# One adaLN block on one Trainium2 core: first modulation summed on TensorE, second group's norm and transposes placed among the first heads' maxima, first stores reordered

## The chip, the cores and the metric

The program runs on one core of one Trainium2 chip. The metric is device time in microseconds (us) of one execution; lower is better. Before the change the median of three timed runs is 696.45 us (694.09 to 696.74). The profile shown here is of one further execution.

## The reference

For 2048 tokens of width 448, sixteen heads of 28 and a feed-forward width of 1792, in float32:

```python
mod = (_silu(c) @ w_mod).reshape(c.shape[0], 6, 1, -1)
sa, ca, ga, sb, cb, gb = ...
h = _layernorm(x, axis=-1) * (1 + ca) + sa
x = x + ga * _A_ref(h, A_wqkv, A_wo)      # causal attention, window 256
h = _layernorm(x, axis=-1) * (1 + cb) + sb
x = x + gb * _B_ref(h, B_w1, B_b1, B_w2)  # Dense -> Mish -> Dense
```

## The kernel before, in words

Tokens are worked on in four groups of 512. Every float32 product is made of three fast products: each operand is split into a rounded high part and the remainder (tiles `hh` and `hl` for the normalized tokens, `wq` and `wql` for the weights), and a projection of one tile is eleven matmuls (`passes`, lines 210 to 214).

**The start (lines 400 to 503).** SyncE (SP) issues all loads in one queue: the tokens of group 0, the modulation weights `wm` in two halves (columns 0 to 255 and 256 to 447, four pieces each), and the projection weights in three parts. VectorE (DVE) takes the statistics of the norm. GpSimd (POOL) and DVE then form the first modulation: `sums` (lines 405 to 412) multiplies each piece of `wm` by its column of `sT`, the silu of the condition, and adds it to `acc`; `mods` (lines 414 to 419) turns the sum into columns by four matmuls against ones for each half; `mods_out` copies them to `cols`. Meanwhile TensorE (PE) transposes the normalized tokens (line 441), and `warmup` (line 466) fills gaps with matmuls whose result nobody uses: 8 and 12 of them. ScalarE (ACT) and DVE apply `cols` and split (`hT_hi`, `hT_lo`), and 33 matmuls on line 486 make the first three tiles of q and k, which are stored to DRAM (`scr`). The modulation of the second half is made after the first nine of these.

**The first heads' maxima (lines 993 to 1006).** Heads are loaded back from `scr` as `q` and `k` (`L`). `A` (line 646) makes a head's scores for 128 queries into one of two buffers `sA`, and DVE takes their row maximum into `mx` (line 655). A maximum is needed before a unit `B` (line 679), which makes scores again with the maximum folded in and lets ACT take the exponential into `P` (line 700); `PV` (line 702) multiplies by v. `M2` (line 659) transposes the maxima of two heads (`mt`, line 661), DVE splits them (`mr`), and a small DMA writes them into `q`. In the first stretch `A` runs for heads 0 to 3, four times each, between the matmuls of a generator, `fill_main(0)`: the v tiles first, then the tiles 1, 5, 2 and 6 of q and k. Heads 2 and 3 also step `side`, whose first content is the norm of group 1 (`ln1[1]`). DVE works in order, so statistics and normalization stand between the maxima.

**The units (lines 1008 to 1056).** 192 units follow, 48 for each group of queries. Unit u issues `B(u)`, up to two `A` of the next four heads, loads (`load_slot`), and as many matmuls of the generator as `RATE[g]` us of credit pay for; `FRONT[g]` doubles the credit of the first units. In the order that the program takes, units 0 to 10 of group 0 hold no projection matmul, only the four transposed chunks of group 1 (`gen_hT(1)`, four transposes each). At a group's end what is left of the generator is issued in one piece (line 1014). DMAs that wait in `later` are issued one by one in some units; tiles `st` that carry q and k to the stores come from four buffers (tag `qs`).

Of the kernel before, what the change touches and what calls it, by code (L numbers as in the profile page):

```python
# [8 lines left out]
F32 = mybir.dt.float32  # L9
F32R = mybir.dt.float32r  # L10
# [41 lines left out]
def adaln_block(ctx: ExitStack, tc: tile.TileContext, x, wqkv, wo, w1, b1, w2, c, w_mod, out):  # L52
# [32 lines left out]
    def bank(tag, bufs, name):  # L85
        return PS[0].tile([128, 512], F32, name=name, tag=tag, bufs=bufs)
# [20 lines left out]
    acc01 = st0.tile([112, 2, D], F32, name="acc01")  # L107
# [186 lines left out]
    def gen_hT(g):  # L294
        drain(ln1[g])
        hh, hl = HT[g] = new_T(g, mid)
        for ci in range(4):
            p = bank("mm", 2, f"tr{g}{ci}")
# [32 lines left out]
        return cost(m, p.shape[-1])  # L331


    later = []

    def flush():
        while later:
# [8 lines left out]
    def qk_out(g, m, p, st=None):  # L346
        st = st or qk.tile([128, 2, GT], F32R, name=f"st{g}_{m}", tag="qs", bufs=4)
        r0, gs = m * 128, slice(g * GT, (g + 1) * GT)
        qn = min(max(D - r0, 0), 128)

        def hi():
            ACT.activation(st[:, 0], p, AF.Copy)

        def lo():
            DVE.tensor_tensor(st[:, 1], p, st[:, 0].bitcast(F32), op=ALU.subtract)
# [25 lines left out]
        return passes(*HT[g], wq3[:, :, ms], wql[:, :, ms])  # L381

    def gen_qkv(g, tiles):
        first = {"v2": ("sB", 2), "v3": ("sB", 2), 1: ("pv", 1), 5: ("tr", 1)} if g == 0 else {}
        for m in tiles:
            p = bank(*first.get(m, ("mm", 2)), f"qk{g}_{m}")
            if isinstance(m, str):
                t = int(m[1])
                hh, hl = HT[g]
                ts = slice(t * 128, (t + 1) * 128)  # L390
                ps = passes(hh[:, :, ts], hl[:, :, ts], wq3[:, :, VS], wql[:, :, VS])
                w = yield from tile_mms(p[:, 0:D], [(b, a) for a, b in ps])
# [9 lines left out]
    nm0 = qk.tile([128, 4], F32, name="nma0")  # L402
    XS[0] = [xin0[:, t] for t in range(4)]

    def sums(h, ks):
        cs = HALF[h][0]
        for k in ks:
            w, o = wm01[k][:, :, cs], acc01[:, :, cs]
            if k == 0:
                POOL.tensor_scalar(o, w, sT[:, 0:1], None, op0=ALU.mult)  # L410
            else:
                DVE.scalar_tensor_tensor(o, w, sT[:, k:k + 1], o, op0=ALU.mult, op1=ALU.add)

    def mods(h):
        for ci in HALF[h][1]:
            n = 128 if ci < 3 else 64
            for i in range(2):
                PE.matmul(pm[0:n, 4 * i + ci:4 * i + ci + 1], acc01[:, i, ci * 128:ci * 128 + n], ones[:, 0:1],
                          start=True, stop=True, skip_group_check=True)

    def mods_out(h):
        for i in range(2):
            if h == 0:
                DVE.tensor_scalar(cols[:, i, 0:2], pm[:, 4 * i:4 * i + 2], float(i), None, op0=ALU.add)
            else:
                DVE.tensor_scalar(cols[:, i, 2:3], pm[:, 4 * i + 2:4 * i + 3], float(i), None, op0=ALU.add)
                for r0 in (0, 64):
                    DVE.tensor_scalar(cols[r0:r0 + 64, i, 3:4], pm[0:64, 4 * i + 3:4 * i + 4], float(i), None,
                                      op0=ALU.add)

    def wq_split(part, cis, eng):
        c0, c1 = QCOLS[part]
        for ci in cis:
            split_hi(wqs[ci][:, c0:c1], wq3[:, ci, c0:c1], ACT)
        for ci in cis:
            split_lo(wqs[ci][:, c0:c1], wq3[:, ci, c0:c1], wql[:, min(ci, 2), c0:c1], ci, eng)

    def trs_of(cis):
        for t in (0, 2, 1, 3):
            for ci in cis:  # L440
                PE.transpose(trs[ci][:, t * 128:(t + 1) * 128], XS[0][t][:, ci * 128:(ci + 1) * 128], ident)
# [6 lines left out]
    DVE.scalar_tensor_tensor(nm0, mv0[:, :, 0], -1.0, rs0, op0=ALU.mult, op1=ALU.mult)  # L448
    sums(0, (0,))
    for t in (0, 1):  # L450
        ACT.activation(xin0[:, t, 0:D], xin0[:, t, 0:D], AF.Identity, scale=rs0[:, t:t + 1], bias=nm0[:, t:t + 1])
    for t in (2, 3):
        DVE.tensor_scalar(xin0[:, t, 0:D], xin0[:, t, 0:D], mv0[:, t, 0:1], rs0[:, t:t + 1],
                          op0=ALU.subtract, op1=ALU.mult)
    for t in (0, 2, 1, 3):
        dup(XS[0][t])
    sums(1, (0,))
    sums(0, (1, 2, 3))
    pm = bank("sA", 2, "mc01")
    trs = [bank(("sB", "mm")[ci // 2], 2, f"tr0{ci}") for ci in range(4)]  # L460
    hh, hl = HT[0] = new_T(0, mid)
    warm = bank("pv", 1, "warm")

    def warmup(n):
        for _ in range(n):
            PE.matmul(warm[:, 0:384], identr, mask, start=True, stop=True, skip_group_check=True)

    trs_of((0, 1))
    warmup(8)
    mods(0)  # L470
    trs_of((2, 3))
    warmup(12)
    wq_split(0, (0, 1), POOL)
    sums(1, (1, 2))
    mods_out(0)
    for ci in (0, 1):
        hT_hi(trs[ci], ci, hh, 0)
    hT_lo(trs[0], 0, hh, hl, 0)
    sums(1, (3,))
    hT_lo(trs[1], 1, hh, hl, 0)  # L480
    wq_split(0, (2, 3), POOL)
    first = [(m, bank(tag, b, f"qk0_{m}"), qk_passes(0, m)) for m, tag, b in ((0, "pv", 1), (3, "tr", 1), (4, "sA", 2))]
    for lo_n, hi_n in ((0, 3), (3, 6), (6, 9), (9, 11)):
        for m, p, ps in first:
            for n in range(lo_n, hi_n):
                PE.matmul(p, ps[n][1], ps[n][0], start=(n == 0), stop=(n == 10))
        if lo_n == 0:
            mods(1)
            mods_out(1)
            for ci in (2, 3):  # L490
                hT_hi(trs[ci], ci, hh, 0)
                hT_lo(trs[ci], ci, hh, hl, 0)
            wq_split(1, range(4), DVE)
    x_load(1)
    st01 = {}
    for m, p, ps in first:
# [6 lines left out]
    wq_split(2, range(4), POOL)  # L503
    st0_s.close()
    att, att_s = pool("att")

# [398 lines left out]

    def fill_main(g):
        if g == 0:
            yield from gen_qkv(0, VT + (1, 5, 2, 6))
        if g + 1 < NG:
            yield from gen_hT(g + 1)  # L910
# [78 lines left out]
    def fill0(n):  # L989
        for _ in range(n):  # L990
            pipe.step()
            next(fillers[0])
    need({f"v{t}" for t in range(4)}, 0)
    for i in range(4):
        for t in range(4):
            if t % 2 == 0:
                fill0((4, 1, 1, 0)[i] if t == 0 else 1)
            A(i, t)
            if i >= 2:
                side_step(0, False)  # L1000
        if i % 2:
            fill0(1)
            M2(i // 2)
            if i == 1 and 0:
                rest()
            load_slot(3 + i)
            load_slot(4 + i)
    NU = 3 * NS
    credit = 0.0
    for u in range(NU + 7):  # L1010
# [17 lines left out]
        if r in (7, 11) and 4 * q + 4 < NS:  # L1028
            M2(2 * q + 2 + (r == 11))
        for a in range(4):  # L1030
            if (u - (8, 11, 14, 16)[a]) % 12 == 0 and u >= (8, 11, 14, 16)[a]:
                load_slot(4 * ((u - (8, 11, 14, 16)[a]) // 12) + 8 + a)
        if r - 3 in (0, 1) and 0 <= (u - 12 - 3) // 12 < NS // 4:
            (E, E2)[r - 3](q - 1)
        if g < NG:
# [8 lines left out]
            if v > 1:  # L1044
                side_step(g, len(tiles) > 1)
            if later and r in (1, 4, 5, 6, 8, 9):
                later.pop(0)()
        if u == NU:
            drain(fillers[NG - 1], side[1])
# [105 lines left out]
```

## Time and profile before

| what | value |
|---|---|
| median of three runs | 696.45 us (694.09 to 696.74) |
| the profiled execution's own time | 694.23 us |
| its span, first to last instruction | 692.5 us |
| PE busy | 660.0 us, 95% of the span |
| DVE busy | 349.5 us, 50% |
| ACT busy | 279.3 us, 40% |
| POOL busy | 97.4 us, 14% |
| mean granted TensorE clock | 0.978 |

The busy times are shares of the whole span. The change touches the first 140 us and the order around units 96 to 143, so those stretches are read for themselves. A PE that is busy all the time can still be slow: the granted clock is a column of its own.

### The profile page before, as it was taken

The page shows a single profiled execution, that of the slowest core. Times are in us where ns is not written, and L with a number is a line of the kernel's source. Part 1 is how long each engine was busy: PE and PEld are TensorE (multiplying, and loading weights), DVE is VectorE, ACT ScalarE, POOL GpSimd, SP SyncE. Part 2 cuts the span into 40 slices and gives each one's busy share as a digit, 9 for nine tenths or more (in the row PEclk, how much of TensorE's full clock was granted, in tenths as well). Part 3 has the DMA queues.
Part 4 walks back from the last instruction along what each step waited for, and adds up shares of the span by engine and source line. Part 5 has one row for each costly group of instructions (what it writes and reads, how often), then busy time and mean ns, then how long its engine had stood idle before and what let it go on. Part 6 is the DMA issues. An engine that isn't in the chain of part 4 may idle for free.

```text
span 692.5 us, 10958 instructions
## 1 busy us (share of the span) xinstructions
PE 660.0 (95%) x3925; PEld 521.2 (75%) x3925; DVE 349.5 (50%) x944; ACT 279.3 (40%) x478; POOL 97.4 (14%) x148
## 2 busy tenths in 40 slices
PE   4988999999999999999998999999999999999996
PEld 3765766777777677777665788888888888888885
DVE  6855476565578666577678433335133323241112
ACT  2514444474452644345455752342233223322321
POOL 7413000043000300000001064321000000000002
PEclk9995799999999999999999999999999999999999
DMA  8766465656755566446563564103000200010001
GB/s 222 206 183 228 128 194 191 208 143 213 223 174 153 155 203 214 166 125 199 157 198 109 153 194 121 53 1 107 0 1 1 81 27 1 0 41 13 1 1 53
DMA packets 49586, 83.80 MB, mean 121 GB/s; under 512 B 6254, under 2 KB 28028, under 8 KB 49532
## 3 DMA queue, kind: packets, MB, share of 16 engines
q1 hardware_dynamic: 49532, 83.10, 39.5%
q8 instruction: 31, 0.51, 0.3%
q14 instruction: 23, 0.19, 0.1%
HBM read 53.45 MB, written 29.36 MB: 120 GB/s over the span
## 4 chain that ended last, share of the span: by engine, by line
PE 76%; issue 11%; DVE 5%; DMA 5%; ACT 1%; POOL 1%; SPq 1%; POOLq 0%; DVEq 0%; ACTq 0%
PE z L882 16%; PE qk L326 9%; PE sA L653 6%; PE pv L710 6%; PE sB L697 5%; PE qk_v L326 5%; PE wo L326 5%; PE acc L1075 5%; PE acc L1076 5%; PE acc L1074 5%; PE sB L695 4%; DMA k<-scr 3%; DVE junk L655 2%; PE et L721 1%; PE trf L259 1%
## 5 line engine op out<-in xcount | busy, mean ns | idle before, releaser
L655 DVE CUSTOM_DVE_ANT_0 junk<-sA,mask 128x384 bf16<-128x384 f32 (+2 forms) x256 | 135.4, 529 | 95.3 <-PE sA L653 82.7
L700 ACT ACTIVATE P<-sB 128x512 f32<-128x512 f32 (+2 forms) x192 | 109.1, 572 | 140.4 <-PE sB L697 136.7
L890 DVE TENSOR_TENSOR al<-t,ah 128x512 fp32r<-128x512 f32 x56 | 38.8, 692 | 201.0 <-ACT ah L889 201.0
L888 ACT ACTIVATE t<-z,b1c 128x512 f32<-128x512 f32 x56 | 38.5, 687 | 188.2 <-PE z L882 177.3
L653 PE MATMUL sA<-k,q 84*128 84x384 f32 (+2 forms) x256 | 93.1, 373 | 10.4 <-DVE mx L655 7.1
L697 PE MATMUL sB<-q,k 86*128 86x384 f32 (+1 forms) x352 | 92.8, 338 | 1.1 <-DMA q<-mr 1.0
L882 PE MATMUL z<-hhf,w 128*128 128x512 f32 x224 | 89.8, 401 | 0.0
L882 PE MATMUL z<-hlf,w 128*128 128x512 f32 x224 | 88.8, 396 | 0.0
L1074 PE MATMUL acc<-w2h,ah 128*128 128x448 f32 x224 | 82.1, 367 | 0.0
L1075 PE MATMUL acc<-w2l,ah 128*128 128x448 f32 x224 | 82.1, 367 | 0.0
L1076 PE MATMUL acc<-w2h,al 128*128 128x448 f32 x224 | 82.0, 366 | 0.0
L882 PE MATMUL z<-hhf,w1l 128*128 128x512 f32 x168 | 66.4, 395 | 0.0
L653 PEld LDWEIGHTS sA<-k,q 84*128 84x128 f32 x256 | 50.0, 198 | 20.3 <-DVE mx L655 16.6
L695 PEld LDWEIGHTS <-identr 128*128 128x128 bf16 x320 | 22.2, 101 | 53.0 <-issue 50.2
L695 PE MATMUL sB<-fdmask,identr 128*128 128x128 bf16 (+1 forms) x320 | 61.7, 259 | 0.2 <-ACT P L700 0.2
L697 PEld LDWEIGHTS sB<-q,k 86*128 86x128 f32 x352 | 57.4, 200 | 2.2 <-DMA q<-mr 1.2
L710 PE MATMUL pv<-P,v 128*32 128x256 f32 (+2 forms) x704 | 50.8, 403 | 0.0
L882 PEld LDWEIGHTS z<-hlf,w 128*128 128x128 f32 x224 | 42.3, 189 | 9.8
L882 PEld LDWEIGHTS z<-hhf,w 128*128 128x128 f32 x224 | 42.3, 189 | 8.8 <-issue 0.6
L1074 PEld LDWEIGHTS acc<-w2h,ah 128*128 128x128 f32 x224 | 42.1, 188 | 5.3
L1075 PEld LDWEIGHTS acc<-w2l,ah 128*128 128x128 f32 x224 | 42.1, 188 | 5.2
L1076 PEld LDWEIGHTS acc<-w2h,al 128*128 128x128 f32 x224 | 42.0, 188 | 3.6
(152 smaller groups left out, 988.9 us busy)
## 6 DMA issues: line engine op xcount, KB each, us to landing
k<-scr SPq DMA_DIRECT2D x48, 252.0 KB
scr<-st SPq DMA_DIRECT2D x22, 512.0 KB
q<-scr SPq DMA_DIRECT2D x64, 168.0 KB
scr<-st SPq DMA_DIRECT2D x30, 256.0 KB
x<-x1d SPq DMA_DIRECT2D x10, 448.0 KB
xin<-in_A_x_dram SPq DMA_DIRECT2D x8, 448.0 KB
xr<-in_A_x_dram SPq DMA_DIRECT2D x16, 224.0 KB
x1d<-xr SPq DMA_DIRECT2D x16, 224.0 KB
```

The lines of the kernel that those rows point to most:

```text
L326: PE.matmul(p, b, a, start=(n == 0), stop=(n == 10))
L653: PE.matmul(p[:, c0:384], q[0:84, t * 128:(t + 1) * 128], k[0:84, t * 128 + c0:t * 128 + 384], start=True, stop=True)
L655: DVE.tensor_tensor_reduce(out=junk[:, c0:384], in0=p[:, c0:384], in1=mask[:, c0:384], scale=1.0, scalar=-3.0e38, op0=ALU.add, op1=ALU.max ...
L695: PE.matmul(p[:, c:c + n], identr, fdmask[:, m:m + n], start=(i == 0), stop=False, skip_group_check=True)
L697: PE.matmul(p[:, c:c + 128 * (t1 - t0)], k[:, jj * 128:(jj + 1) * 128], q[:, t0 * 128:t1 * 128], start=False, stop=True, skip_group_check= ...
L700: ACT.activation(P[:, c0:], p[:, c0:], AF.Exp, scale=SCALE)
L710: PE.matmul(pvb[q][32 * a:32 * a + 32, t0 * 128:t1 * 128], V[j % NV][:, h + a, :], Pt[4 * w + a][:, c:c + 128 * (t1 - t0)], start=(b == 0 ...
L882: PE.matmul(zb[n], ps[m][1], ps[m][0], start=(m == 0), stop=(m == 10))
L890: DVE.tensor_tensor(al[n], t, ah[n].bitcast(F32), op=ALU.subtract)
L1074: PE.matmul(p, ah[n][:, ts], w2h[f], start=(f == 0), stop=False)
L1075: PE.matmul(p, ah[n][:, ts], w2l[f], start=False, stop=False)
L1076: PE.matmul(p, al[n][:, ts], w2h[f], start=False, stop=(f == NF - 1))
```

## The change

Five things are done.

1. The first modulation is accumulated in PSUM: `mods(h, ks)` multiplies the pieces of `wm` directly by the columns of `sT`, 16 matmuls of one column for each half in place of 4, and `sums` and the tile `acc01` are gone. The matmuls of the second half stand ahead of the first projection. The 20 warming matmuls become 6.
2. ACT normalizes three of the first group's four tiles (two before); the lower parts of the projection weights' second part are made by POOL (DVE before); the first v tile takes its passes in another order.
3. The norm of group 1 is taken on ACT in place of DVE, its statistics stand ahead of the first maximum, and its four chunks (transposes, from buffers of `sB`) stand among the tiles 1, 5, 2 and 6. Group 0's `hh` and `hl` move to the tag `on`.
4. The stores of tile 5 are cut in two, rows 0 to 31 first; stores are flushed inside the first heads' maxima; loads and stores of the units get other slots.
5. `RATE[2]` goes from 0.93 to 0.83 and `FRONT[2]` from 3 to 2: of group 2's matmuls (units 96 to 143), 40 are left to the drain in unit 143 in place of 14.

```diff
-    def sums(h, ks):
-        cs = HALF[h][0]
+    def mods(h, ks):
         for k in ks:
...
-                PE.matmul(pm[0:n, 4 * i + ci:4 * i + ci + 1], acc01[:, i, ci * 128:ci * 128 + n], ones[:, 0:1],
-                          start=True, stop=True, skip_group_check=True)
+                    PE.matmul(pm[h][0:n, 4 * i + ci:4 * i + ci + 1], wm01[k][:, i, ci * 128:ci * 128 + n], sT[:, k:k + 1],
+                              start=(k == i == 0 and ci == HALF[h][1][0]), stop=(k == 3), skip_group_check=True)
...
-    trs_of((0, 1))
-    warmup(8)
-    mods(0)
-    trs_of((2, 3))
-    warmup(12)
+    mods(0, (0, 1))
+    trs_of(0, (0, 1))
+    trs_of(1, (0, 1))
+    mods(0, (2, 3))
+    for t in (2, 3):
+        trs_of(t, (0, 1))
+    for t in range(4):
+        trs_of(t, (2, 3))
...
+    warmup(6)
...
+            if ci == 0 and x == 0:
+                mods(1, range(4))
+                mods_out(1)
...
         def store():
-            later.append(put)
+            later.append(put_first if (g, m) == (0, 5) else put)
...
-            yield from gen_qkv(0, VT + (1, 5, 2, 6))
+            yield from gen_qkv(0, VT)
+            chunk["v"] = 3
+            tiles, chunks = gen_qkv(0, (1, 5, 2, 6)), gen_hT(1)
+            n = 0
+            for _ in tiles:
+                if n in (6, 8, 9, 15):
+                    next(chunks)
+                n += 1
+                yield
...
-    RATE = (0.68, 1.01, 0.93, 0.45)
-    FRONT = (0, 1, 3, 0)
-    ln1 = {g: gen_ln1(g) for g in range(1, NG)}
+    RATE = (0.68, 1.01, 0.83, 0.45)
+    FRONT = (0, 1, 2, 0)
+    ln1 = {g: gen_ln1(g, g == 1) for g in range(1, NG)}
...
+    for _ in range(8):
+        side_step(0, False)
+    fill0(1)
     for i in range(4):
         for t in range(4):
-            if t % 2 == 0:
-                fill0((4, 1, 1, 0)[i] if t == 0 else 1)
             A(i, t)
+            fill0((1, 1, 0, 1)[i])
+            if i * 4 + t < 6 or i * 4 + t == 11:
+                flush()
```

The rows below are the order in which the built program issues instructions on one engine; rows that repeat are counted (x4). First PE from the program's first matmul, before the change: `tr` are transposes of the normalized tokens `xin`, `mc` the modulation's columns.

```order
L441 MATMUL tr_224<-ident,xin_85 128x128
L441 MATMUL tr_225<-ident,xin_85 128x128
...
L466 LDWEIGHTS identr
L466 MATMUL warm<-mask,identr 128x384
...
L418 MATMUL mc_223<-ones,acc_94 128x1 x4
L441 MATMUL tr_226<-ident,xin_85 128x128
...
L486 MATMUL qk_0_290<-hh_228,wq_88 128x512
```

And the same place after it, up to the first projection:

```order
L416 MATMUL mc_218<-sT,wm_0_90 128x1 x4
L416 MATMUL mc_218<-sT,wm_1_91 128x1 x4
L439 MATMUL tr_220<-ident,xin_85 128x128
...
L416 MATMUL mc_218<-sT,wm_2_92 128x1 x4
L416 MATMUL mc_218<-sT,wm_3_93 128x1 x4
...
L466 MATMUL warm<-mask,identr 128x384
L416 MATMUL mc_219<-sT,wm_0_90 128x1 x2
L416 MATMUL mc_219<-sT,wm_0_90 64x1 x2
...
L504 MATMUL qk_0_281<-hh_224,wq_88 128x512
```

PE now starts with the modulation itself, and all of both halves stands ahead of the first projection (`qk_0`).

Next PE around the maxima of heads 2 and 3, before: `sA` are the scores, `qk_6` a tile of group 0's own projection.

```order
L653 MATMUL sA_2_586<-k_2_382,q_1_397 128x384
L653 MATMUL sA_3_592<-k_2_382,q_1_397 128x384
L653 MATMUL sA_0_601<-k_3_383,q_1_397 128x128
L653 MATMUL sA_1_604<-k_3_383,q_1_397 128x256
L326 MATMUL qk_6_562<-hl_229,wq_88 128x512
L326 MATMUL qk_6_562<-hh_228,wq_88 128x512
L326 MATMUL qk_6_562<-hl_229,wq_88 128x512
L653 MATMUL sA_2_612<-k_3_383,q_1_397 128x384
L653 MATMUL sA_3_617<-k_3_383,q_1_397 128x384
L259 MATMUL tr_629<-ident,xin_350 128x128 x4
```

After, from the transpose `mt` of the maxima of heads 0 and 1 on:

```order
L677 MATMUL mt_597<-ident,mx_513 8x128
L669 MATMUL sA_0_609<-k_2_385,q_1_400 128x128
L669 MATMUL sA_1_612<-k_2_385,q_1_400 128x256
L669 MATMUL sA_2_615<-k_2_385,q_1_400 128x384
L669 MATMUL sA_3_618<-k_2_385,q_1_400 128x384
L669 MATMUL sA_0_621<-k_3_386,q_1_400 128x128
L325 MATMUL qk_2_572<-hh_224,wq_88 128x512
L325 MATMUL qk_2_572<-hh_224,wql 128x512
L325 MATMUL qk_2_572<-hl_225,wq_88 128x512
L669 MATMUL sA_1_630<-k_3_386,q_1_400 128x256
L325 MATMUL qk_2_572<-hh_224,wq_88 128x512
```

The transposes of group 1 have left this place; three of its four chunks stand ahead of it. Five scores of heads 2 and 3 follow each other, and projection matmuls stand between the later ones.

Last DVE at the same place, before: `sta` and `mva` are the statistics of group 1, `xin` its normalization, and the row that only reads the accumulated maximum is the one without a source.

```order
L655 ISA junk,mx_567<-sA_2_586,mask 128x384
L655 ISA mx_567 128x1
L219 BN_STATS sta_589<-xin_350 128x6
L220 BN_AGGR mva_571<-sta_589 128x2
L655 ISA junk,mx_567<-sA_3_592,mask 128x384
...
L249 TENSOR_SCALAR xin_350<-xin_350,mva_571,rsa_598 128x448
L655 ISA junk,mx_567<-sA_2_612,mask 128x384
```

After:

```order
L354 TENSOR_TENSOR st_5_566<-qk_5_530,st_5_566 128x512
L679 CAST mr_599<-mt_597 8x128
L680 TENSOR_TENSOR mr_599<-mt_597,mr_599 8x128
L671 ISA junk,mx_608<-sA_0_609,mask 128x128
L671 ISA mx_608 128x1
L671 ISA junk,mx_608<-sA_1_612,mask 128x256
L671 ISA mx_608 128x1
L671 ISA junk,mx_608<-sA_2_615,mask 128x384
```

Statistics and normalization no longer stand between the maxima.

More of the change, by code (lines that the diff above doesn't have):

```diff
@@ L331, in tile_mms @@
         return cost(m, p.shape[-1])
-    later = []
+    later, late = [], []
     def flush():
@@ L357, in store, with put_first @@
         def store():
-            later.append(put)
+            later.append(put_first if (g, m) == (0, 5) else put)
+        def put_first():
+            put_rows(0, 5, st, ((0, 32, 1, 0),))
+            late.append(lambda: put_rows(0, 5, st, ((32, 128, 1, 0),)))
+            done.add((g, m))
         def put():
@@ L383, in gen_qkv @@
     def gen_qkv(g, tiles):
[L384 removed]
+        first = {"v2": ("sB", 2), "v3": ("sB", 2), 1: ("pv", 1), 6: ("pv", 1)} if g == 0 else {}
         for m in tiles:
@@ L403, in adaln_block @@
     XS[0] = [xin0[:, t] for t in range(4)]
-    def sums(h, ks):
-        cs = HALF[h][0]
+    def mods(h, ks):
         for k in ks:
[L408 to L418, printed above, removed]
-                          start=True, stop=True, skip_group_check=True)
+            for ci in HALF[h][1]:
+                n = 128 if ci < 3 else 64
+                for i in range(2):
+                    PE.matmul(pm[h][0:n, 4 * i + ci:4 * i + ci + 1], wm01[k][:, i, ci * 128:ci * 128 + n], sT[:, k:k + 1],
+                              start=(k == i == 0 and ci == HALF[h][1][0]), stop=(k == 3), skip_group_check=True)
     def mods_out(h):
@@ L447, in adaln_block @@
         POOL.tensor_tensor(rs0[:, h], rs0[:, h], mhalf[:, h], op=ALU.pow)
[L448 to L455, printed above, removed]
+    for h in (slice(0, 2), slice(2, 4)):
+        DVE.scalar_tensor_tensor(nm0[:, h], mv0[:, h, 0], -1.0, rs0[:, h], op0=ALU.mult, op1=ALU.mult)
+        for t in range(4)[h]:
+            xn0(t)
+    for t in range(4):
         dup(XS[0][t])
-    sums(1, (0,))
-    sums(0, (1, 2, 3))
-    pm = bank("sA", 2, "mc01")
+    pm = [bank("sA", 2, f"mc{h}") for h in range(2)]
     trs = [bank(("sB", "mm")[ci // 2], 2, f"tr0{ci}") for ci in range(4)]
-    hh, hl = HT[0] = new_T(0, mid)
+    hh, hl = HT[0] = [mid.tile([128, 4, GT], F32R, name=f"h{n}0", tag="on", bufs=2) for n in "hl"]
     warm = bank("pv", 1, "warm")
@@ L502, in adaln_block @@
     put_rows(0, 4, st01[4], ((0, 48, 1, 0),))
-    wq_split(2, range(4), POOL)
+    for c in range(4):
+        if c not in (0, 1, 2, 3):
+            wq_lo(1, c, DVE)
+    for c in range(4):
+        wq_hi(2, c)
+        wq_lo(2, c, POOL)
     st0_s.close()
@@ L1001, in adaln_block @@
         if i % 2:
-            fill0(1)
             M2(i // 2)
-            if i == 1 and 0:
-                rest()
             load_slot(3 + i)
             load_slot(4 + i)
+    later[:0] = late
     NU = 3 * NS
@@ L1043, in adaln_block @@
                 credit -= step(g)
-            if v > 1:
+            if v > 1 and u > 8:
                 side_step(g, len(tiles) > 1)
-            if later and r in (1, 4, 5, 6, 8, 9):
+            if later and r in (1, 3, 4, 5, 6, 9):
                 later.pop(0)()
```

77 lines of the change are left out of this document (45 added, 32 removed).

## The prediction

> **What bounds the kernel now.** I read the page's busy times and slices first, then a table of busy time by stage, then the waits of PE in the weak stage, the chain of waits, and the order of time at the start. The page's first section and its row of granted clock:
>
> ```profile
> PE 660.0 (95%) x3925; PEld 521.2 (75%) x3925; DVE 349.5 (50%) x944; ACT 279.3 (40%) x478; POOL 97.4 (14%) x148
> PEclk9995799999999999999999999999999999999999
> ```
>
> PE bounds the kernel, and the granted clock is low in two of the 40 slices, near the span's tenth. So time is to be won where PE idles or runs slowly, not by taking work from others. Busy time by stage; the columns are the stretch in us, its length, then busy time and instructions of PE, of weight loads (PEld), DVE, ACT and POOL, then PE's granted clock and the DMA:
>
> ```profile
> 10.30:19.40 9.10, 8.55 (x47) 5.83 (x47) 7.56 (x11) 3.80 (x7) 6.51 (x9) 1.00 0.84 220
> 37.20:46.00 8.80, 8.79 (x40) 6.95 (x40) 4.02 (x15) 1.74 (x3) 0.32 (x1) 1.00 0.81 248
> 46.00:50.90 4.90, 3.64 (x16) 2.23 (x14) 3.87 (x15) 0.60 (x1) 0.00 (x0) 1.00 0.13 46
> 50.90:54.30 3.40, 1.60 (x6) 0.98 (x6) 3.19 (x12) 0.15 (x1) 0.32 (x2) 1.00 1.04 375
> 54.30:58.40 4.10, 2.48 (x7) 1.07 (x7) 3.30 (x11) 0.44 (x1) 2.09 (x5) 0.50 0.63 189
> 58.40:78.40 20.00, 19.81 (x88) 14.35 (x86) 9.27 (x39) 11.12 (x20) 5.07 (x4) 0.50 0.38 132
> ```
>
> At 50.9 to 54.3 PE issues 6 matmuls and DVE is busy nearly throughout; then the clock falls to half and stays there to 78.4, although PE shows as busy. The waits of PE from 40 to 62 us (us in total, times, longest):
>
> ```profile
> PE sA L653 <- DVE mx L655: 2.6, 3, 1.5
> PE tr L259 <- DVE xin L249: 1.5, 3, 0.6
> ```
>
> PE waits for the maxima, and these stand behind the statistics and the normalization in DVE's queue. How much the half clock costs is seen in the exponentials of the units, one row of ACT's line 700 for each unit (stretch, length, busy time and count, clock, DMA):
>
> ```profile
> 58.40:78.40 20.00, 5.88 (x12) 0.50 0.38 132
> 78.40:97.00 18.60, 5.89 (x12) 1.00 0.66 200
> 97.00:129.40 32.40, 9.38 (x20) 1.00 0.71 233
> 129.40:136.80 7.40, 2.39 (x4) 1.00 0.27 88
> 136.80:148.30 11.50, 4.59 (x8) 1.00 0.60 155
> ```
>
> Twelve units almost without projection matmuls (four, at the end) take 20.0 us at half clock; the next twelve take 18.6 us with some 35 of them. So that work is nearly free there at full clock.
>
> **The change part by part. The start.** The chain of waits gives the unit prices (start, us, what, count); the projections of tiles 0, 3, 4 (line 486) end and the v tiles begin at 28.32, and v ends at 37.4:
>
> ```profile
> 21.26 0.68 PE mc L418 x8
> 25.02 3.30 PE qk L486 x13
> 28.32 9.08 PE qk_v L326 x44
> 37.40 4.42 PE qk L326 x19
> 45.83 0.56 DVE junk L655
> 46.54 0.56 DVE junk L655
> 53.39 3.16 DMA k<-scr
> 63.82 0.87 PE tr L259 x4
> 136.77 0.44 PE tr L259 x4
> ```
>
> A projection matmul costs 4.42/19 = 0.233 us, a v matmul 9.08/44 = 0.206, a transpose 0.11 at full clock and 0.22 at half. PE's first work in order of time (start, us, what, count):
>
> ```profile
> 12.05 2.11 PE L466 MATMUL warm<-mask,identr 128*128 128x384 bf16 x8
> 14.23 1.05 PE L418 MATMUL mc<-ones,acc 112*128 112x1 f32 x8
> 16.05 2.11 PE L466 MATMUL warm<-mask,identr 128*128 128x384 bf16 x12
> 18.31 0.48 PE L486 MATMUL qk<-hh,wq 128*128 128x512 f32 x1
> ```
>
> The first 8 warming matmuls take as long as the next 12: 0.26 against 0.18 us. PE starts slow here, whatever the clock column shows before the first recorded change. Four modulation matmuls leave 8 records of 0.12 us. They stream one column, so the weight load must set that time, and I let it double with the clock as a transpose does: 0.22. SP issues the second half's pieces of `wm` as the first half's land:
>
> ```profile
> 7.40 0.33 SPq L59 DMA_DIRECT2D wm<-in_w_mod_dram  x1
> 10.16 0.31 SPq L59 DMA_DIRECT2D wm<-in_w_mod_dram  x1
> ```
>
> So after the change PE can begin at 7.4 and no longer waits for sums. But its queue ahead of the first projection is long: 32 records (7.0 us at 0.22), 16 transposes (3.4 at half clock), 6 warming matmuls (2.1 at 0.35, twice the later ones' time) and 32 records of the second half, half of them 64 wide (0.68/8 = 0.085 each at full clock, 0.17 at half: 2.7 to 5.4). That ends at 22.6 to 25.3. The 33 projections take 7.7 us, and some 8 of them run at half clock first (+1.6). The v tiles then begin at 31.9 to 34.6, against 28.3. If the clock is full from the start, the same list gives 3.9 + 1.8 + 1.1 + 2.7 + 7.7 = 17.2 us from 7.4, so 24.6. I take **+5 us (−3.7 to +7)**, nearer the slow end because nothing in that list but six matmuls resembles the work after which the clock rose.
>
> [...]
>
> POOL's four lower parts (about 1.2 us each in place of DVE's) end before the third group of v passes, which the new order of passes puts last; DVE's gain lets the first stores start earlier, but their loads are not waited for. Both are nought; without this cover each is worth under 1 us.
>
> **The heads' maxima, to unit 12.** From the end of v at 37.4 to unit 12 at 78.4 is 41.0 us now. After: 28 projection matmuls (6.5), 8 scores (0.6 a head, 1.2), 12 transposes (1.3) make 9.0 us. Heads 2 and 3 are then bound by DVE. By form, at full clock:
>
> ```profile
> L655 DVE CUSTOM_DVE_ANT_0 junk<-sA,mask 128x384 bf16<-128x384 f32 x32 | 17.7, 554 | 10.3 <-PE sA L653 8.6
> L655 DVE CUSTOM_DVE_ANT_0 junk<-sA,mask 128x256 bf16<-128x256 f32 x8 | 3.4, 420 | 3.3 <-PE sA L653 3.3
> L655 DVE CUSTOM_DVE_ANT_0 junk<-sA,mask 128x128 bf16<-128x128 f32 x8 | 2.3, 288 | 5.0 <-PE sA L653 4.7
> L355 DVE TENSOR_TENSOR st<-qk,st 128x512 fp32r<-128x512 f32 x7 | 4.8, 687 | 0.0
> ```
>
> Two wide maxima start 46.54 − 45.83 = 0.71 apart, 0.16 above the row's 0.55; so a head takes 0.71 × 2 + 0.58 + 0.45 = 2.45, two heads 4.9, and one lower part of a store 0.7 stands ahead: 5.7 us with the turn-round. Twelve units follow; they hold 33 projection matmuls and fewer PV than the twelve at 78.4, so 18.6 − 1.5, and 0.7 for the late maxima of heads 2 and 3: 17.8. Sum 32.5, so **−8.5 us at full clock**.
>
> But five scores follow each other there, and PE does about 0.6 us of work in 2.8. Six matmuls in 3.4 us brought the fall at 54.3; 16 in 4.9 us did not at 50.9. I expect the clock to fall in most executions, and to return soon, since eleven dense projections follow: one stretch like 3.4 us at half clock, worth 1.7, taken as **+1.5 (0 to +11)**. Loads of heads 4 to 7 now stand behind fewer stores; the stores of tile 5 stand behind the maxima of heads 2 and 3, and a load lands 3.2 us after its issue (the DMA row above), about when head 6 is due: 0 (to +2).
>
> **Units 12 to 48.** Now 136.8 − 78.4 = 58.4 us. Group 1's projections end in unit 42 instead of 47, so 31 units at 32.4/20 = 1.6 us and 5 without filler at 11.5/8 = 1.4, less a little since group 0's are narrower: 49.6 + 6.5 = 56. **−2.5 (−4 to 0).**
>
> **Group 2.** 26 more matmuls of 0.206 fall into the drain: +5.3 us there. If the units they leave are bound by PE, these give it back; three more units near 98 to 105 are left without filler. **+0.5 (−1 to +5.3).** Groups 1 and 3 keep their order on PE: 0.
>
> Sum: 5 − 8.5 + 1.5 − 2.5 + 0.5 = −4 us. The profiled execution took 694.23, so **690 us**. That execution is 2.2 us below the median of 696.45. The sum is made against it and not scaled; half a per cent of the median, 3.5 us, is about what a measurement of this kernel can tell from no change.
>
> **The rivals.** (1) PE's clock rises during the new early work. For it: the matmuls begin 3 us sooner. Against: one-column matmuls hardly stream. The start is then −3.7 instead of +5: 690 − 8.7 = 681.
>
> (2) The gain is eaten: the start costs 7, and group 2's drain its 5.3 because the units before it are bound by DVE and ACT. For it: eight units without filler take 11.5 us, hardly less than units with. 690 + 2 + 4.8 = 697. Against: both must be at their ends.
>
> (3) Slower: the clock falls at heads 2 and 3 and stays half through the first twelve units, as it did from 54.3 to 78.4 though PE was busy. Half of a like stretch of 24 us, less the 1 or so already in the sum, is 11 more: 701. It decides by whether units with about 3 projection matmuls each are dense enough; before, units without any were not, and the clock came back 1.6 us after the first such matmuls at 76.7:
>
> ```profile
> 77.09 1.50 PE qk L326 x4
> 78.72 0.23 PE sB L697
> ```
>
> That these matmuls now stand in every unit from the first speaks against it.
>
> [...]
>
> **How the numbers follow.** Forecast 0.57, rival 1 0.14, rival 2 0.20, rival 3 0.09. The forecast's own band is 686 to 694, of which about four fifths lie below 693.0 (faster by over 0.5%): faster 0.61, with rival 1. Same (693.0 to 699.9) is rival 2 and the rest of the forecast: 0.30. Slower is rival 3: 0.09. The range takes in rivals 1 and 2, 681 to 697; rival 3 and tails are left out.
>
> **What would show it.** The exponentials of units 0 and 12 start now, in ACT's order of time, at:
>
> ```profile
> 59.94 0.48 ACT L700 ACTIVATE P<-sB 128x384 f32<-128x384 f32 x1
> 79.04 0.49 ACT L700 ACTIVATE P<-sB 128x384 f32<-128x384 f32 x1 [1.52 <-PE sB L697]
> ```
>
> Right: v begins later than 28.3, the warming rows and the projections show half pace near 20 to 26; those two rows stand near 58 and 77, by the same sum; the clock column holds no 20 us of 0.50. Wrong: v begins before 28 (the start's price), the clock column at half for more than two stretches of 3.4 us between 45 and 75 (the gap), or the stretch of units 96 to 144 longer than now by over 2 us (the drain).

## The result, and the profile after

In 20 executions of each kernel the changed one takes 698.24 us in the median and the kernel before 694.03: ratio 1.0059, 95% interval 1.0035 to 1.0083. It is slower by 0.6%, about 4 us. The forecast was 690 with a range of 681 to 697. The profiled execution of the changed kernel took 697.66 us (span 695.9, against 692.5), so it stands for the median; its difference of 3.4 us is what has to be explained.

The page of the changed kernel, its row of busy times and its row of granted clock:

```profile
PE 664.5 (95%) x3959; PEld 529.4 (76%) x3959; DVE 339.2 (49%) x930; ACT 283.0 (41%) x483; POOL 97.8 (14%) x152
PEclk9899999999999999999998999999999999999999
```

The long stretch of half clock near the span's tenth is gone (5 and 7 before; now 8 or more everywhere), and DVE has 10 us less to do. The first is as forecast; the time still went up. So the next view is one that tells where in the program the distance between the two kernels changes. The exponential of each unit is one row of ACT (line 700 before, 716 after); the table subtracts their start times in the profiled executions.

| unit | before, us | after, us | after minus before |
|---|---|---|---|
| 0 | 59.94 | 59.66 | -0.27 |
| 12 | 79.04 | 77.05 | -1.99 |
| 42 | 126.44 | 124.10 | -2.34 |
| 48 | 136.87 | 130.99 | -5.88 |
| 54 | 145.91 | 143.66 | -2.25 |
| 96 | 226.72 | 224.39 | -2.32 |
| 132 | 294.86 | 289.14 | -5.72 |
| 150 | 326.35 | 328.46 | +2.11 |
| 168 | 354.78 | 356.98 | +2.20 |
| 191 | 387.16 | 391.02 | +3.86 |

Up to unit 48 the change wins nearly 6 us. It loses 3.6 in the next six units, 4.4 between units 96 and 150, and 1.7 behind unit 168. Two rows of ACT's order of time, units 0 and 12 after the change:

```profile
59.66 0.49 ACT L716 ACTIVATE P<-sB 128x384 f32<-128x384 f32 x1 [2.95 <-PE sB L713]
77.05 0.49 ACT L716 ACTIVATE P<-sB 128x384 f32<-128x384 f32 x1 [0.81 <-PE sB L713]
```

**The start.** The chain of waits of the changed kernel (start, us, what, count):

```profile
7.61 3.55 PE mc L416 x16
11.16 0.96 PE tr L439 x4
12.12 3.20 PE mc L416 x16
15.32 2.66 PE tr L439 x12
17.98 1.03 PE warm L466 x6
19.01 3.82 PE mc L416 x32
22.83 9.37 PE qk L504 x29
```

The early modulation matmuls take 0.22 us each and the transposes 0.22, against 0.12 and 0.11 at full clock before: half pace. The warming matmuls take 1.03/6 = 0.17 each, so in this execution they run at full pace from the first, behind 12 transposes (0.18 for the later ones before). The second half's 32 records take 0.12, and then this order of time of PE shows half pace again (0.43 from one projection to the next; the granted clock is 0.50 from 21.4 to 28.2), then full (0.23):

```profile
26.33 0.63 PE L504 MATMUL qk<-hl,wq 128*128 128x512 f32 x1
26.76 0.63 PE L504 MATMUL qk<-hh,wq 128*128 128x512 f32 x1
...
30.66 0.39 PE L504 MATMUL qk<-hl,wq 128*128 128x512 f32 x1
30.89 0.39 PE L504 MATMUL qk<-hh,wq 128*128 128x512 f32 x1
...
32.93 0.36 PE L325 MATMUL qk_v<-wq,hh 128*128 128x448 f32 x1
```

The v tiles begin at 32.93 instead of 28.3.

**The end of group 1's projections.** In the order of time of PE and of the DMA queue (SP) near unit 50:

```profile
134.72 0.34 PE L711 MATMUL sB<-fdmask,identr 128*128 128x128 bf16 x2
134.82 0.48 PE L713 MATMUL sB<-q,k 86*128 86x384 f32 x2
137.25 0.51 PE L669 MATMUL sA<-k,q 84*128 84x384 f32 x1 [1.96 <-DMA k<-scr]
```

```profile
130.97 1.36 SPq L59 DMA_DIRECT2D q<-mr  x2
132.43 0.41 SPq L59 DMA_DIRECT2D q<-scr  x1
132.89 0.38 SPq L59 DMA_DIRECT2D k<-scr  x1
```

The first score of head 21 waits for its load, which is issued at unit 47 behind the rows of the maxima. Units 42 to 48 have no filler left and take 6.89 us instead of 10.43, so the load, unmoved in units, comes too late in time. The clock falls behind the wait, to 0.50 from 137.4 to 140.8; busy time in the stretch (length, PE, weight loads, DVE, ACT, POOL, clock, DMA):

```profile
131.00:137.40 6.40, 4.37 (x41) 2.94 (x39) 3.12 (x10) 5.32 (x9) 2.54 (x2) 1.00 0.48 128
137.40:143.70 6.30, 6.30 (x42) 4.63 (x43) 3.56 (x11) 3.01 (x6) 1.63 (x2) 0.73 0.60 154
```

This is one of several; the waits of PE over the whole span, first before, then after (us in total, times, longest):

```profile
PE sA L653 <- DVE mx L655: 7.1, 13, 1.5
PE sA L653 <- DMA k<-scr: 2.5, 4, 1.1
```

```profile
PE sA L669 <- DMA k<-scr: 8.0, 8, 2.0
PE sA L669 <- DVE mx L671: 5.2, 13, 1.1
```

The maxima are waited for less, the loads more.

**The end of group 2's projections.** The stretches between the exponentials of units 96, 132, 144 and 150, first before, then after:

```profile
226.72:294.86 68.14, 67.03 (x498) 49.94 (x496) 42.25 (x138) 34.05 (x58) 5.52 (x5) 1.00 0.58 185
294.86:318.00 23.14, 22.77 (x182) 17.84 (x183) 17.40 (x52) 9.89 (x19) 0.00 (x0) 1.00 0.51 137
318.00:326.35 8.35, 8.01 (x76) 5.70 (x69) 6.69 (x22) 5.13 (x10) 1.58 (x3) 1.00 0.90 250
```

```profile
224.39:289.14 64.75, 62.48 (x472) 45.41 (x470) 42.67 (x138) 32.70 (x55) 5.49 (x5) 1.00 0.63 195
289.14:317.58 28.44, 28.20 (x207) 22.45 (x209) 16.65 (x50) 11.48 (x20) 0.00 (x0) 1.00 0.41 112
317.58:328.46 10.88, 9.55 (x76) 7.03 (x69) 7.61 (x24) 5.18 (x10) 1.63 (x3) 0.84 0.75 220
```

In the first stretch PE has 26 matmuls fewer and is 3.4 us shorter. The second has 25 more and is 5.3 longer. The third has the same 76 instructions, and is 2.5 longer at a clock of 0.84. What stands at its begin, in PE's order of time after the change:

```profile
316.70 0.37 PE L325 MATMUL wo<-wo,hlo 128*128 128x448 f32 x1
316.91 0.34 PE L711 MATMUL sB<-fdmask,identr 128*128 128x128 bf16 x2
...
320.88 0.44 PE L669 MATMUL sA<-k,q 84*128 84x384 f32 x1 [1.06 <-DVE mx L671]
```

A score waits 1.1 us for a maximum, and the clock drops behind that (0.51 from 321.7 to 325.1). Why DVE is late is seen in its own order of time: it adds each finished tile of the output to rows of `x` (the tile `xr`, line 622), and the maxima stand behind these sums in its queue.

```profile
316.67 0.62 DVE L622 TENSOR_TENSOR xr<-xr,wo 128x448 f32<-128x448 f32 x1 [2.61 <-DMA xr<-in_A_x_dram]
318.88 0.62 DVE L622 TENSOR_TENSOR xr<-xr,wo 128x448 f32<-128x448 f32 x1 [0.71 <-DMA xr<-in_A_x_dram]
320.29 0.53 DVE L671 CUSTOM_DVE_ANT_0 junk<-sA,mask 128x384 bf16<-128x384 f32 x1
```

The 40 projections of unit 143 are most of four output tiles, made in 8.3 us. SP loads the rows of `x` for the last two of them at 311.95 and 316.12, while the row of projections is already running, and DVE waits 3.3 us for them. Before the change no such sum waits for its rows. So this too is a load that has become late.

### The profile page after: what moved, and what is told of

The parts are those of the page before. It is cut to its first block, busy times and chain, and to the rows that moved or that the text cites. A ratio compares the mean times of both kernels' runs of the same rounds, so it can differ in the third digit from the quotient of the medians.

```text
span 695.9 us, 11033 instructions
## 1 busy us (share of the span) xinstructions
PE 664.5 (95%) x3959; PEld 529.4 (76%) x3959; DVE 339.2 (49%) x930; ACT 283.0 (41%) x483; POOL 97.8 (14%) x152
## 4 chain that ended last, share of the span: by engine, by line
PE 74%; issue 11%; DMA 8%; DVE 5%; SPq 1%; ACT 1%; POOL 0%; POOLq 0%; DVEq 0%; ACTq 0%
PE z L898 15%; PE qk L325 9%; PE sA L669 6%; PE pv L726 5%; PE sB L713 5%; PE acc L1102 5%; PE acc L1103 5%; PE acc L1104 5%; DMA k<-scr 4%; PE sB L711 4%; PE qk_v L325 4%; PE wo L325 4%; DVE junk L671 2%; PE mc L416 2%; PE qk L504 1%
## 5 line engine op out<-in xcount | busy, mean ns | idle before, releaser
L713 PE MATMUL sB<-q,k 86*128 86x384 f32 (+1 forms) x352 | 91.1, 334 | 1.6 <-DMA q<-mr 1.6
```

The costliest lines, as they stand in the source:

```text
L713: PE.matmul(p[:, c:c + 128 * (t1 - t0)], k[:, jj * 128:(jj + 1) * 128], q[:, t0 * 128:t1 * 128], start=False, stop=True, skip_group_check= ...
```

## The experiments

Each time is a median, each ratio one to the kernel before on the same chip; that kernel's own median was 693.6 to 694.5 each time. The ratios are not quotients of these medians and can differ from them by up to 0.4%. The changed kernel's 698.24 is from the first occasion, so differences to it carry the spread between occasions too.

**Group 2's two numbers undone.**

```diff
-    RATE = (0.68, 1.01, 0.83, 0.45)
-    FRONT = (0, 1, 2, 0)
+    RATE = (0.68, 1.01, 0.93, 0.45)
+    FRONT = (0, 1, 3, 0)
```

> The changed kernel with group 2's two numbers as they were (RATE 0.93, FRONT 3). Theory A, the drain: the 26 matmuls that the new numbers leave for the end of group 2 cost PE time that the units before them don't give back; by the two profiles units 96 to 150 are 4.4 us longer after the change, so this kernel takes 698.2 - 4.4 = 693.8 us, a ratio of about 1.000 to the kernel before, and the distance to before at unit 150 is -2.3 as at unit 96. Theory B, interaction: the loss belongs to what else has moved (the earlier units, clock windows), and the numbers alone do little: 697 us or more, ratio 1.004 or more.

Measured: 691.25 us, ratio 0.9969 (0.9942 to 0.9996), so 7.0 under the changed kernel. In the profile the distance to before is -1.98 at unit 96 and -2.48 at unit 150, as theory A had it. The two profiled executions are 7.8 us apart: 4.9 of it lies between units 96 and 150, and 3.3 behind unit 168, where this execution shows no half clock. The latter can be chance. The start was 1.7 us earlier at unit 0 (v tiles at 31.45), but nothing of that is left at unit 96.

**The same two numbers alone, in the kernel before.** The edit is the reverse, on the kernel before.

> The kernel before with only group 2's two numbers changed (RATE 0.83, FRONT 2). Theory A: 4.4 us slower, about 698.4 us, ratio 1.006, all of it between the exponentials of units 96 and 150, and some 40 projection matmuls of wo in a row near unit 143. Theory B: under 1.5 us, ratio under 1.002.

Measured: 698.98 us, ratio 1.0072 (1.0037 to 1.0108). Between units 96 and 150 the profile loses 4.3 us (+0.11 to +4.42), in the same pieces as above:

```profile
226.82:291.50 64.68, 62.44 (x472) 45.42 (x470) 42.78 (x138) 32.66 (x55) 5.50 (x5) 1.00 0.61 195
291.50:319.67 28.17, 28.04 (x207) 22.45 (x209) 17.12 (x51) 11.57 (x21) 0.00 (x0) 1.00 0.44 121
319.67:330.76 11.09, 9.58 (x76) 6.42 (x69) 7.15 (x22) 5.16 (x9) 1.63 (x3) 0.85 0.68 198
```

So this part alone costs 4.7 us, with none of the rest of the change present. Theory B falls. Here too DVE stands idle for 2.7 us ahead of the fourth output tile's sum, which starts at 321.14 after a load of `x` issued at 318.42; that it waits for this load is read from the times, since the profile names another releaser.

**The old start in the changed kernel.** Sums on DVE and POOL and 20 warming matmuls, as before, and with them the old norm of group 0 and the lower parts of the weights' second part on DVE; all else as changed.

```diff
-    mods(0, (0, 1))
-    trs_of(0, (0, 1))
...
+    trs_of((0, 1))
+    warmup(8)
+    mods(0)
+    trs_of((2, 3))
+    warmup(12)
```

> The changed kernel with the start of the kernel before (sums on DVE and POOL, 20 warming matmuls), everything else as after the change. Theory A, the price of the start stays where it falls: v tiles begin at 28.3 instead of 32.9, and the 4.6 us reach the end: 693.6 us, ratio 1.000. Rival, given back: the heads' maxima then wait for DVE or for the first loads, so that unit 0 is earlier by less than 2 us and the end by less still: 696.5 us or more, ratio 1.004 or more.

Measured: 694.36 us, ratio 1.0001 (0.9968 to 1.0034), 3.9 under the changed kernel. In its profile unit 0 is 4.5 us earlier than after the change, and 3.4 of them are left at the last unit. The rival falls. Both starts vary with the execution: with the old one the v tiles begin at 27.8 to 30.9 us in the nine profiles of this study that have it, with the new one at 31.5 to 36.1 in four. The 36.1 is an execution (that with the old load units, below) whose clock did not come up behind the transposes: its six warming matmuls take 2.13 us.

**One load a unit earlier.** The second head of each four is loaded at unit 10 of the pattern instead of 11, ahead of the rows of the maxima.

```diff
-            if (u - (8, 11, 15, 15)[a]) % 12 == 0 and u >= (8, 11, 15, 15)[a]:
-                load_slot(4 * ((u - (8, 11, 15, 15)[a]) // 12) + 8 + a)
+            if (u - (8, 10, 15, 15)[a]) % 12 == 0 and u >= (8, 10, 15, 15)[a]:
+                load_slot(4 * ((u - (8, 10, 15, 15)[a]) // 12) + 8 + a)
```

> The changed kernel with every fourth head's second load (heads 9, 13, 17, 21 and so on) one unit earlier. Theory C, the load: units 42 to 48 got shorter by 3.5 us with the change, units 48 to 54 longer by 3.6, since a score waits 2.0 us for k and the clock falls for one 3.4 us stretch behind that wait; with the load a unit (about 1.1 us) earlier the wait falls to about 1 us and the clock may stay full: 1 to 3 us less, 695 to 697 us. Rival: the transfer ends when it did, since its queue or its buffer is not free before, or the time comes back in the next unit: 698 us, no change.

Measured: 690.24 us, ratio 0.9956 (0.9923 to 0.9990): 8 us under the changed kernel (7 by the two ratios), more than any theory had. The waits of PE in this kernel:

```profile
PE sB L713 <- DMA q<-mr: 5.9, 6, 2.0
PE sA L669 <- DVE mx L671: 4.2, 12, 0.7
PE sA L669 <- DMA k<-scr: 0.3, 1, 0.3
```

The waits on k are gone (8.0 to 0.3), those on the maxima's rows, which now stand behind the load, grew (1.6 to 5.9), DVE is waited for 1.0 less: 4.4 in all. One half-clock stretch of 3.4 us fewer (six for seven) is 1.7 more. That makes 6.1 of the 6.3 us between the two profiled executions (697.66 and 691.38); the rest between the medians isn't explained.

By units, the gain does not lie where theory C looked for it. The missing half-clock stretch is one at the start, and 0.8 us are won before unit 0. Units 48 to 54 still take 12.16 us: in place of the wait on k a unit waits 1.5 us for the maxima's rows, and the clock falls behind that as it does after the change, where it is 0.73 in the 6.3 us behind the wait. The largest piece, 2.5 us, comes in units 144 to 150: they take 8.35 us, as in the kernel before, although the row of 40 projections is still there. The second head's load no longer stands in the queue between the maxima's rows and the first output tile's store; the last two loads of `x` are issued 2.8 and 4.5 us behind the first projection of the row (3.4 and 7.6 after the change), and DVE's sums there wait for PE alone:

```profile
DVE xr L622 <- PE wo L325: 3.0, 4, 0.8
```

**Is it the other two loads?** The change also moved the third and fourth heads' loads from units 14 and 16 to 15 and 15; here that alone is undone.

> The changed kernel with the loads of the third and fourth head of each four back at units 14 and 16 (the change has 15 and 15). Theory D: the third head's load, issued a unit later, is what scores wait for (waits of scores on k are 7.3 us in the profile after, 2.5 us before): they fall by 2 us or more and the time to 696 us or less. Rival: the second head's load at unit 11 is the late one, as its move by one unit took all those waits away; the old numbers change nothing: 697 to 699 us.

Measured: 698.78 us, ratio 1.0060 (1.0034 to 1.0086), k still waited for 7.9 us. Theory D falls. After the change the five longest waits on k are all for second heads (21, 33, 37, 57 and 61); with the old units the longest are for heads 21 (2.7 us), 59, 37 and 61. The profiled execution took 702.94 us, the longest of its twelve; against the profile after the change it loses 3.2 us before the v tiles.

**The same earlier load in the kernel before** (10 for 11 in its own list).

> The kernel before with only the second head's load one unit earlier (10 for 11). Theory C2: the late loads came with the change, as units 43 to 50 got free of filler; before, scores waited 2.5 us for k in all, so 1 to 2.5 us less here, 692 to 693.5 us, ratio 0.996 to 0.998, against 0.9897 between the changed kernel and its version with the earlier load (690.24 over the median of 698.24 on another occasion). Rival: the earlier load helps either kernel alike, by other means than those waits: 6 us or more, 688 us or less.

Measured: 693.80 us, ratio 1.0004 (0.9970 to 1.0039). No gain can be told. The load became worth moving only with the change.

**The middle part alone.** The kernel before with the second group's norm and chunks among the maxima, the outputs' buffers for the first chunks, the new order of v's first passes and the order of the first stores; its own start, group 2 numbers and load units.

> The kernel before with only the middle part of the change (second group's norm and chunks among the first heads' maxima, first chunks in the outputs' buffers, order of the first stores); the start, group 2's numbers and the load units are those of before. By the prediction's terms for this part (-8.5, +1.5, -2.5): 694.2 - 9.5 = 684.7 us. Theory A, additive: the changed kernel with the old start took 694.4, less 4.4 for group 2's numbers: 690.0 us, ratio 0.994. Rival: what is won to unit 48 is lost at the next heads' loads, whatever the start: 693 us or more, ratio 0.998 or more.

Measured: 690.83 us, ratio 0.9941 (0.9914 to 0.9968). Additive, to a microsecond. It is 3.7 us faster than before, and not the 9.5 of the prediction's terms: by its profile unit 48 is 9.7 us earlier than before, unit 54 only 6.1, with head 21 waiting 1.9 us for k again. So the rival's mechanism is there too, but it takes back only a part.

**The second half's modulation mixed among the projections** (the changed kernel). What stood behind the 32 records, the copy of their columns and the splits of the last two chunks and of the weights' second part, now stands behind the last of the mixed ones.

```diff
+    mixed = [mods_of(1, range(4))]
...
             for n in range(lo_n, hi_n):
                 PE.matmul(p, ps[n][1], ps[n][0], start=(n == 0), stop=(n == 10))
+                if mixed and next(mixed[0], 0) == 0:
```

> The changed kernel with the second half's 32 one-column records one instruction after each of the first 16 projections of the first tiles, not all ahead of them. Theory E, the clock: the records stream nothing, so with all in a row the clock falls for two stretches (21.4 to 28.2 us) and the projections after them run at half pace; mixed, PE streams about half of the time and the clock stays full: v tiles begin at about 31.6 instead of 32.9 us, since the third chunk then waits some 1.5 us, and the time falls by 1.3 us to about 697. Rival: the clock falls just the same, since half is not enough: v begins at 33 to 35 us, 698 to 700 us.

Measured: 703.42 us, ratio 1.0131 (1.0093 to 1.0169). The v tiles begin at 38.2. Worse than either theory; PE's order of time:

```profile
25.40 0.48 PE L499 MATMUL qk<-hh,wql 128*128 128x512 f32 x1
25.81 0.28 PE L420 MATMUL mc<-sT,wm 112*64 112x1 f32 x2
26.02 0.49 PE L499 MATMUL qk<-hl,wq 128*128 128x512 f32 x1
...
28.10 0.77 PE L499 MATMUL qk<-hl,wq 128*128 128x512 f32 x1
28.81 0.37 PE L420 MATMUL mc<-sT,wm 112*64 112x1 f32 x2
29.11 0.79 PE L499 MATMUL qk<-hh,wq 128*128 128x512 f32 x1
```

and its clock by stretch:

```profile
17.80:27.00 9.20, 9.05 (x45) 5.85 (x44) 2.08 (x3) 0.99 (x3) 2.56 (x3) 1.00 0.87 251
27.00:37.20 10.20, 9.47 (x25) 6.27 (x24) 3.66 (x10) 3.30 (x6) 4.24 (x4) 0.50 0.00 1
```

At full clock a projection and its two records took 0.46 us with records 128 wide, but 0.62 with those 64 wide. Then the clock fell at 27, with PE busy for all but 0.15 of the 9.2 us ahead, and stayed down for 10 us, though from 30.7 on only projections ran, with two waits of 0.4 us for the late splits. Of the delay of v, 0.9 us come from the warming matmuls, which ran at half pace in this execution (2.13 us in place of 1.23). Theory E's remedy falls: the clock fell with the records mixed in as well.

**The combination**: middle part, old start, group 2's old numbers, the earlier load.

> Middle part of the change with the start and group 2's numbers of before, and the second head's load one unit earlier (units 8, 10, 15, 15). Additive: 694.4 - 4.4 - 8.0 = 682.0 us, ratio 0.982. With overlap (part of what the earlier load saved was in group 2's end, which is undone here): 684 to 687. Rival: the waits only change their name, since PE has the same matmuls to do and the maxima's rows then stand behind the load in the queue: 689 us or more.

Measured: 684.78 us, ratio 0.9863 (0.9829 to 0.9897); the case with overlap. It differs from the middle part alone in the loads' units only (8, 10, 15, 15 for 8, 11, 14, 16) and is 6.0 us faster.

**Two small edits on it**, one by one and together: RATE 0.97 for group 2, and the old order of v's first passes.

> The combination (middle part of the change, old start, group 2's numbers of before, second head's load one unit earlier) with RATE 0.97 for group 2: no projection matmul is left for unit 143, against 14 at 0.93 and 40 at 0.83. Theory A, the drain has a price per matmul: 26 more cost 4.4 to 4.7 us, 0.17 us each, so 14 fewer give 2.4 us: 682.4 us, ratio 0.983. Rival, a threshold: the first 14 are hidden beside the exponentials as the scores go on, only a long row stops DVE and ACT: 684 to 685.5, no change.

> The combination with the passes of v's first tile in their old order: with the old start, the new order asks first for the lower part that DVE splits last, and PE waited 0.5 us for it. Theory: 0.5 us less at the v tiles and at the end, 684.3 us, not told from no change in the time, but the wait of qk_v on wq is gone from the profile. Rival: the wait moves to the first stores.

> The combination with both small edits: the passes of v's first tile in their old order and RATE 0.97 for group 2 (no projection matmul left for unit 143). Theory A, a price per drained matmul: 0.5 us of wait and 14 x 0.17 = 2.4 us less than the combination's 684.8: 681.9 us, and units 96 to 150 shorter than the combination's by about 2 us. Threshold rival: units 96 to 150 as in the combination with the old order, about 684 us or as that one measured.

Measured: 682.61 (0.9859, 0.9804 to 0.9913), 682.17 (0.9861, 0.9802 to 0.9920) and 681.88 us (0.9817, 0.9782 to 0.9851); by the medians all three are at 0.983. None of the three can be told from the combination by its interval. The wait of qk_v on wq is gone with the old order. Whether the last 14 drained matmuls have a price stays open: units 96 to 150 take 103.86 us in the combination, 100.70 with RATE 0.97, but 100.02 with the old order of passes alone, which doesn't touch them, and 99.85 with both. The combination's longer time lies in units 96 to 132, where its clock fell for one stretch (at 230.7; projections 0.43 us apart from 231.1 on), not at the drain. The last kernel has the lowest median here, 1.5 to 2.2% under the kernel before by its interval.

## Why the prediction was wrong, point by point

Three steps of the sum failed. Group 2 was put at +0.5 and measured 4.4. Units 48 to 54 had no term and cost 3.6, because loads issued a fixed number of units ahead came late. What lies behind unit 168 had none either and cost 1.7. The terms up to unit 48 came out.

**The start (+5, from -3.7 to +7): right.** 4.6 us in the profile, 3.9 in the experiment, v inside the 31.9 to 34.6. The record prices were right too (0.22 at half pace). Rival 1's time is out. One step inside was off: in the profiled execution the clock was up behind the transposes, since the warming matmuls run at 0.17 at once and not at the 0.35 of the list. But behind the 32 records it was down again, and 13 projections ran at half pace (0.43), not the 8 that the author had estimated. In two other executions the six warming matmuls take 1.7 us in place of 1.2, so the clock came up among them; in the one with the old load units projections run at half pace until 31 us, though the same twelve transposes ran; so the agreement of the start's time is in part luck.

**The maxima, to unit 12 (-8.5 and +1.5): right.** From the v tiles to unit 12 it takes 77.05 - 32.93 = 44.1 us instead of 79.04 - 28.32 = 50.7: -6.6 against -7. Inside, two errors cancel: unit 0 came at 59.66 and not near 58, and the twelve units took 17.4 us and not 19. The clock fell, and for one stretch of 3.4 us (0.50 from 55.5 to 58.9; the profile before has one of that length too, 0.50 from 368.3 to 371.7):

```profile
56.20 0.63 PE L325 MATMUL qk<-hh,wq 128*128 128x512 f32 x1
56.63 0.63 PE L325 MATMUL qk<-hh,wql 128*128 128x512 f32 x1
...
59.46 0.40 PE L325 MATMUL qk<-hh,wq 128*128 128x512 f32 x1
```

The fall came in six of the eleven profiles that have the middle part, each time for one stretch. Rival 3, the clock down through twelve units, did not come in any of them. After the change the longest wait of PE ahead of it was 0.7 us, and in the mixture above the clock fell with PE idle for 0.15 us of the 9.2 ahead; so in these executions a fall came without a long wait.

**Units 12 to 48 (-2.5, from -4 to 0): right, and the step behind it is missing.** It came to -3.9, since the units without filler take 6.89/6 = 1.15 us and not the 1.4 of the sum. But the sum ended at unit 48 and went on at unit 96, as if what is won at one row were kept at the next. Units without filler pass faster; a load that is issued a fixed number of units ahead is then issued less time ahead. That took back 3.6 us at once. The sum's term for late loads, "0 (to +2)", was asked for heads 4 to 7 alone; the heads at the groups' ends had to be asked too. The earlier load showed it: units 48 to 54 take 9.2 to 9.5 us in the combination and its three variants, and 12.6 to 13.5 in the six profiles with the middle part and the load at unit 11. One profile stands out, the changed kernel with the earlier load, with 12.16: the rows of the maxima landed late there instead, and why they did isn't settled.

**Group 2 (+0.5, from -1 to +5.3): the size was wrong.** 4.4 in the profile and 4.7 alone. The trade of matmuls between units and drain was expected to come out even; the units gave back 3.4, the drain took 5.3. The 2.5 us behind the drain had no term: in the long row of projections the loads of `x` for the last output tiles come late, DVE waits 3.3 us for them, a score waits 1.1 us for DVE, and the clock falls. In the profile with the earlier load of the second head DVE has its rows in time and the 2.5 us are gone, with the same row of projections; so it is the late loads that cost them, and not the row by itself. This was rival 2's place, and its 5.3 is what the drain took; its reason holds in part, since the units did give back 3.4 and the rest was lost behind the drain. That its 697 comes near the measured 698 is in part luck: it has nothing for units 48 to 54 and behind 168, and a dearer start.

**Behind unit 168** another 1.7 us, not foreseen: a wait on k of 1.7 instead of 0.8 (head 61, again a second head), and two stretches of half clock instead of one (0.50 from 369.5 to 376.3, against 368.3 to 371.7). Three of the fourteen profiles show no half clock there, the version without group 2's numbers among them; its cause isn't settled.

Sum of the measured steps: 4.6 - 6.6 - 3.9 + 3.6 + 4.4 + 1.7 = +3.8 at the last unit, 3.86 in the table. The base was right: 694.2 against a median of 694.0 in more runs. By the prediction's own signs, v, unit 12 and the clock column came out as forecast; units 96 to 144 got 1.9 us longer, just under the 2 us that were to prove it wrong, because the rest of that loss fell into the six units behind.

## What to carry to other kernels

A gain is kept only until the next thing that is scheduled by count and not by time: after pricing what an edit saves, look at each load that is issued a fixed number of steps ahead and ask whether the shortened steps still cover it. Moving filler to the end of a group wasn't an even trade here: 26 matmuls gave back 3.4 us and took 5.3, and the packed output tiles met late loads of their own. Reading only that PE waits for DVE would have missed this; what DVE waits for has to be asked too. And a change made of three parts is worth taking apart: here one was a gain of 3.7 us, two were losses of 3.9 and 4.7, and the gain became 9.7 when the loads' units were moved along with it.

## What the runs showed of the hardware

PE's clock fell behind waits of PE, and also with PE busy. Behind a wait of 1.96 us, with PE busy for 4.37 of 6.40 us, it was 0.50 from 137.4 to 140.8 us. With PE busy for 3.82 of 3.82 us, on 32 one-column matmuls, it fell at 21.4 us, and 13 projections took 0.43 us each behind them. In the mixture one 0.23 us projection to 0.23 or 0.39 us of records, from 20 us on, was followed by a fall within 7 us, with PE busy for 9.05 of 9.20 us. Behind twelve transposes of 0.22 us in a row the clock was up in the profile after the change, where the warming matmuls take 0.17 us. In the profile with the old load units it wasn't: the warming matmuls take 2.13/6 = 0.36 us there, and projections 0.43 until 31 us. What decides between the two isn't settled here.
